# Decode attention: keys read in runs of 32, one exp a pair, and low parts made by an identity matmul

## The chip, the cores and the metric

The kernel runs on one core of a Trainium2 chip. The metric is the device time of one execution in microseconds, lower is better. Five executions of the kernel before gave 324.24 to 327.63 us, with a median of 326.44 us.

## The reference

Four tokens (B = 4, one query position each) of width 448 go through two identical layers. Each layer is attention over a cached window, then a SwiGLU FFN, both with a layer norm ahead and a residual behind. The caches and the weights are the same in both layers.

```python
B, Sq, D = 4, 1, 448
Hq, Hkv, Sk, Dh = 16, 8, 8192, 256
W = min(4096, max(256, Sk // 4))                       # 2048 keys
q = (x @ wq).reshape(B, Sq, Hq, Dh).transpose(0, 2, 1, 3)
k = jnp.repeat(k_cache[:, :, Sk - W:, :], rep, axis=1)  # rep = 2 query heads a key head
v = jnp.repeat(v_cache[:, :, Sk - W:, :], rep, axis=1)
scores = jnp.einsum("bhqd,bhkd->bhqk", q, k) * (Dh ** -0.5)
o = jnp.einsum("bhqk,bhkd->bhqd", _softmax(scores), v)
A = o.transpose(0, 2, 1, 3).reshape(B, Sq, Hq * Dh) @ wo
Bf = (_silu(x @ w_gate) * (x @ w_up)) @ w_down          # F = 1792

x = x + A(_layernorm(x)); x = x + Bf(_layernorm(x))     # twice
```

All inputs are bf16. For each token and key head the window holds 1 MB of keys and 1 MB of values, so one layer over four tokens reads 64 MB of cache.

## The kernel before

**Pairs and steps.** The unit of work is a pair: one token, one layer, one key head with its two query heads. There are 64 pairs. A window's keys come as two halves of 512 KB, and so do its values; each half is one tile of 128 partitions by 2048 bf16, out of a pool of 27 (`half`). Five of the eight key heads' K and V of a token's first layer stay in the pool until its second layer uses them, so 44 of the 64 pairs load their cache and 20 do not. `steps` joins a pair of one token's second layer with a pair of the next token's first layer for the same head, and the output projection is done once for both.

**A pair, in the order of its data** (function `pair`):

- SP issues the loads of K (L616) and V (L629).
- DVE transposes each K half in place, in 32 x 32 blocks of 32-bit words (L621), so a word holds two neighbouring elements of a key's head dimension.
- GpSimd spreads the query into four masked copies (L646, `qe`).
- TensorE makes the scores (L642, `scores`): 32 matmuls with a stationary operand of 128 x 8 and 128 moving columns, that is 32 keys of each of two by two places in a half. They go to four strips of 32 partitions of a PSUM bank `S` in turn, so a strip holds one quarter of the keys. There are two such banks (NS = 2).
- DVE takes the maximum (L653), TensorE passes it to all strips (L656), DVE reduces it and forms the bias of the exp (L660, L664).
- ScalarE makes the exp out of the bank `S` in two instructions, one for each half of the partitions (L668). They write to different columns of `praw`, and the columns in between stay zero.
- TensorE turns the probabilities so that keys are on partitions (L677, `turn`: 2 matmuls against `selt`), ScalarE copies them to SBUF (L684, `pT`), TensorE sums them (L687) and DVE reduces the sum (L692).
- TensorE multiplies by V (L700, `pv`: 32 matmuls of 256 columns in two halves) into a bank `Y`, columns 256 to 511. There are three such banks (NY = 3).
- Eviction: each result stands on several rows of `Y`, of which some are to carry the bf16 rounding of it and others the remainder. ScalarE copies the whole to bf16 (L712, `oh`). DVE multiplies `oh` by `lomask` and subtracts `Y` (L714), which leaves the negative of the value on some rows and of the remainder on the others.
- TensorE flips and adds the rows (L720, `flip`, against `osel`, which holds the minus sign), DVE multiplies by the inverse of the sum (L725, `oT`), and TensorE adds the projection into a bank `A` (L745, `out_proj`).

At the end of a token's layer come the residual (L563), the norm (L425 to L453), the FFN (gate and up L523, down L551) and, between the layers, the query projection (L482).

**Order.** Nothing is ordered by hand. Every operation is entered into a graph with an engine, a planned duration in us and a rank. `schedule` plays the graph once with these durations and so fixes the order of the instructions on every engine's queue, the order of the loads on SP's queue, and which tile of the pool a load gets. A tile is free again when the last reader is done: the scores for a K half (`o.rel = tuple(kc)`), the matmuls by V for a V half. On the chip each engine takes its queue strictly in this order and waits on semaphores. The planned durations of the operations that matter here:

```python
            o = g.op(PE, 32 * MM, pos - SLEAD, scores, r=tuple(kk) + (f"qe{q_}",), w=(f"s{s_}",), bank=(f"S{s_}",))
```

with MM = 0.034, 0.33 for an exp, 0.08 for the turn, 0.28 for L712 and 0.4 for L714.

Of the kernel before, what the change touches and what calls it, by code (L numbers as in the profile page):

```python
# [6 lines left out]
ALU = mybir.AluOpType  # L7
# [271 lines left out]
def build(nc, A_x, A_k_cache, A_v_cache, A_wq, A_wo, B_x, B_w_gate, B_w_up, B_w_down, out):  # L279
# [3 lines left out]
    with ExitStack() as es:  # L283
# [10 lines left out]
        onesb = sb("onesb", [128, 1], BF16)  # L294
# [3 lines left out]
        selt = sb("selt", [128, 2, 4, 2, 2], BF16)  # L298
# [8 lines left out]
        qmask = sb("qmask", [128, 4], BF16)  # L307
# [13 lines left out]
        pmax = [sb(f"pmax{s}", [128, 1], BF16) for s in range(NS)]  # L321
        praw = [sb(f"praw{s}", [128, 256], BF16) for s in range(NS)]
        pT = [sb(f"pT{s}", [128, 2, 2, 4, 2, 2], BF16) for s in range(NY)]
        oh = [sb(f"oh{s}", [128, DH], BF16) for s in range(NY)]
        osel = sb("osel", [128, 2], BF16)
# [41 lines left out]
        for y in range(2):  # L367
            for x in range(2):
                g.op(DVE, 0.1, R0, lambda e, y=y, x=x: e.tensor_reduce(
                    selt[:, x, :, y, :], ivt[:, :, x, 0:4, :].rearrange("p h a n -> p a n h"), AX.X, ALU.max),  # L370
                    r=("identb",), w=(f"selt{y}{x}",))
# [3 lines left out]
        for s_ in range(NS):  # L375
            g.op(DVE, 0.2, R0, lambda e, s_=s_: e.memset(Sb[s_][:, :], 0.0), w=(f"s{s_}",), bank=(f"S{s_}",))
            g.op(DVE, 0.2, R0, lambda e, s_=s_: e.memset(praw[s_][:, :], 0.0), w=(f"praw{s_}_0", f"praw{s_}_1"))
        for a in range(4):
# [4 lines left out]
            osel[:, :], iv[:, :, 0:2, :].rearrange("p j y n -> p n j y"), AX.XY, ALU.max, negate=True), r=("identb",),  # L383
            w=("osel",))
        g.op(DVE, 0.2, R0, lambda e: e.tensor_reduce(lomask[:, :], iv[:, :, 1, :], AX.XY, ALU.add), r=("identb",),
# [222 lines left out]
        def pair(pos, si, side, nside, t, layer, kvh):  # L608
# [26 lines left out]
            def scores(e):  # L635
                last = None
                for ce in range(8):
                    for hf in range(2):
                        kt = half[kc[hf][0]][:, :].rearrange("p (l g c r v) -> p c v g r l", l=2, g=4, c=4, v=2)
# [10 lines left out]
            o = g.op(PE, 32 * MM, pos - SLEAD, scores, r=tuple(kk) + (f"qe{q_}",), w=(f"s{s_}",), bank=(f"S{s_}",))  # L650
# [16 lines left out]
            for hf in range(2):  # L667
                g.op(SCA, 0.33, pos, lambda e, hf=hf: e.activation(  # L668
                    praw[s_][64 * hf:64 * hf + 40, :].rearrange("p (g r h l) -> p h g r l", g=2, h=2, l=2)[:, hf, :, :, :],
                    Sb[s_][64 * hf:64 * hf + 40, 0:128].rearrange("p (g r l) -> p g r l", g=2, l=2), ACT.Exp,  # L670
                    bias=nb[64 * hf:64 * hf + 40, 0:1]),
                    r=(f"s{s_}", f"nb{s_}"), w=(f"praw{s_}_{hf}",), bank=(f"S{s_}",))

            def turn(e):
                last = None
                for c in range(2):
                    last = e.matmul(Yb[p_][:, 64 + 32 * c:96 + 32 * c], lhsT=praw[s_][0:104, 128 * c:128 * c + 128],  # L677
                                    rhs=selt[0:104, :, :, :, :].rearrange("p x a y n -> p (x a y n)"), start=(c == 0),
                                    stop=False, skip_group_check=True)
                return last  # L680
            g.op(PE, 0.08, pos, turn,
                 r=(f"praw{s_}_0", f"praw{s_}_1") + tuple(f"selt{y}{x}" for y in range(2) for x in range(2)), w=(f"yp{p_}",),
                 bank=(f"Y{p_}",))
# [20 lines left out]
            for hv in range(2):  # L704
# [3 lines left out]
                if not keep_v:  # L708
# [3 lines left out]
            g.op(SCA, 0.28, pos, lambda e: e.activation(oh[p_][:, :], Yb[p_][:, 256:512], ACT.Copy), r=(f"y{p_}",),  # L712
                 w=(f"oh{p_}",), bank=(f"Y{p_}",))
            g.op(DVE, 0.4, pos, lambda e: e.scalar_tensor_tensor(  # L714
                out=oh[p_][:, :], in0=oh[p_][:, :], scalar=lomask[:, 0:1], in1=Yb[p_][:, 256:512], op0=ALU.mult,
# [128 lines left out]
```

## Time and profile before

| | us |
|---|---|
| median of five executions | 326.44 (324.24 to 327.63) |
| the profiled execution's own time | 326.44 |
| its span, first to last instruction | 324.6 |
| TensorE matmuls busy | 238.9 (74%), 5792 instructions |
| TensorE weight loads busy | 168.7 (52%) |
| VectorE (DVE) busy | 198.9 (61%) |
| ScalarE (ACT) busy | 91.1 (28%) |
| GpSimd (POOL) busy | 85.5 (26%) |
| loads' queue, share of the 16 DMA engines | 86.5%, 104.45 MB |
| mean granted TensorE clock | 0.763 |

How to read the lines of the profile: PE is TensorE's matmuls, PEld its weight loads, which overlap them. A matmul's busy time includes its way through the array, so matmuls that follow each other overlap, and a busy PE is not PE at its peak. In the slices the span is cut in 40 equal parts, and a digit is a share in tenths. In the chain, the work that ended last is followed back from the last instruction, at each step to what released it. In the groups, the columns are line, engine, operation, output and inputs, shapes and count, then busy time in us, the mean of one in ns, and the engine's idle time before them with what ended it. SPq is SP's queue, on which all loads are issued.

### The profile page before, as it was taken

Reading aid. Unit: us, or ns where it says so; the run is one execution under the profiler, and the core shown is the slowest. Engines: PE = TensorE matmul, PEld = TensorE weight load, DVE = VectorE, ACT = ScalarE, POOL = GpSimd, SP = SyncE. Lnnn points to the kernel's source line nnn. Section 1 sums busy time; section 2 is a strip of 40 time slices with the busy share of each in tenths; the row PEclk is TensorE's granted clock in tenths of the full one; section 3 lists DMA queues with packets and bytes.
Section 4 is the critical chain, followed back from the end, with each engine's and each line's share of the span. In section 5 each row is a group of like instructions: output and inputs, shape, how many; then the busy total and the mean of one; then the engine's idle time right before and its main releaser. Section 6 shows DMA issues by size and latency. Waiting matters only on the chain.

```text
span 324.6 us, 13161 instructions
## 1 busy us (share of the span) xinstructions
PE 238.9 (74%) x5792; PEld 168.7 (52%) x5792; DVE 198.9 (61%) x744; ACT 91.1 (28%) x289; POOL 85.5 (26%) x199
## 2 busy tenths in 40 slices
PE   2666565456587877688969976799878878689965
PEld 1543333234465545466735644566645547566644
DVE  6397556653145789675547997656567973944422
ACT  0313122111013344223243334222333433124510
POOL 2413211112020333223215232404142324134321
PEclk9998556777556999775597999655759978569965
DMA  7999999999988999998899999999599999736000
GB/s 274 404 404 392 395 396 394 392 397 397 392 319 291 389 372 374 363 365 293 298 367 397 399 380 298 390 389 391 179 397 359 331 388 392 274 103 231 2 2 2
DMA packets 42328, 105.28 MB, mean 324 GB/s; under 512 B 3096, under 2 KB 7200, under 8 KB 41888
## 3 DMA queue, kind: packets, MB, share of 16 engines
q1 hardware_dynamic: 42272, 104.45, 86.5%
q8 instruction: 45, 0.74, 0.9%
q14 instruction: 11, 0.09, 0.1%
HBM read 104.44 MB, written 0.00 MB: 322 GB/s over the span
## 4 chain that ended last, share of the span: by engine, by line
PE 39%; DMA 21%; DVE 16%; SPq 12%; issue 5%; ACT 5%
DMA half<-in_A_v_cache_dram 15%; PE S L642 15%; DVE half L621 8%; PE Y L700 8%; DMA half<-in_A_k_cache_dram 6%; SPq L616 6%; PE Z L482 4%; PE A L745 4%; SPq L629 3%; SPq L398 3%; ACT praw L668 3%; PE Z L523 2%; DVE oh L714 2%; ACT oh L712 1%; PE Y L720 1%
## 5 line engine op out<-in xcount | busy, mean ns | idle before, releaser
L621 DVE STREAM_TRANSPOSE half<-half 128x1024 uint32<-128x1024 uint32 x88 | 108.9, 1239 | 21.0 <-DMA half<-in_A_k_cache_dram 20.8
L642 PE MATMUL S<-half,qe 128*8 128x128 bf16 x2048 | 85.0, 306 | 9.2 <-ACT praw L668 5.0
L700 PE MATMUL Y<-half,pT 128*4 128x256 bf16 x1024 | 54.4, 330 | 20.6 <-DMA half<-in_A_v_cache_dram 12.2
L642 PEld LDWEIGHTS S<-half,qe 128*8 128x8 bf16 x2048 | 51.7, 90 | 28.3 <-ACT praw L668 8.4
L710 POOL TENSOR_TENSOR small<-small 128x2 f32<-128x2 f32 x64 | 44.4, 698 | 78.8 <-DVE small L692 71.5
L668 ACT ACTIVATE praw<-S,small 40x128 bf16<-40x128 f32 x128 | 46.4, 363 | 48.0 <-DVE small L664 46.4
L712 ACT ACTIVATE oh<-Y 128x256 bf16<-128x256 f32 x64 | 24.4, 381 | 86.4 <-PE Y L700 86.0
L646 POOL TENSOR_TENSOR qe<-qc,qmask 128x64 bf16<-128x64 bf16 x64 | 18.7, 294 | 101.0 <-PE S L642 85.1
L653 DVE TENSOR_REDUCE pmax<-S 104x1 bf16<-104x128 f32 x64 | 18.4, 288 | 38.0 <-PE S L642 37.7
L714 DVE SCALAR_TENSOR_TENSOR oh<-oh,small,Y 128x256 bf16<-128x256 bf16 x64 | 30.1, 472 | 17.1 <-ACT oh L712 16.9
L700 PEld LDWEIGHTS Y<-half,pT 128*4 128x4 bf16 x1024 | 21.5, 88 | 28.8 <-DMA half<-in_A_v_cache_dram 14.1
L745 PE MATMUL A<-oT,wo_sb 128*128 128x1 bf16 (+1 forms) x688 | 24.3, 165 | 6.8 <-DVE oT L725 5.1
L745 PEld LDWEIGHTS A<-oT,wo_sb 128*128 128x128 bf16 x688 | 20.9, 99 | 13.1 <-DVE oT L725 7.2
L684 ACT ACTIVATE pT<-Y 128x64 bf16<-128x64 f32 x64 | 13.9, 222 | 42.2 <-PE Y L677 30.1
L720 PE MATMUL Y<-osel,oh 128*128 128x2 bf16 x128 | 12.1, 170 | 13.0 <-DVE oh L714 13.0
L687 PE MATMUL Y<-pT,onesb 128*128 128x32 bf16 x64 | 12.0, 190 | 9.6 <-ACT pT L684 9.5
L720 PEld LDWEIGHTS Y<-osel,oh 128*128 128x128 bf16 x128 | 7.5, 102 | 21.4 <-DVE oh L714 17.1
L449 POOL TENSOR_SCALAR st<-st 128x1 f32<-128x1 f32 x16 | 4.3, 267 | 47.9 <-DVE st L437 36.7
L482 PE MATMUL Z<-xn,wq_sb 128*128 128x1 bf16 (+1 forms) x480 | 15.4, 166 | 1.0 <-DMA wq_sb<-in_A_wq_dram 0.7
L687 PEld LDWEIGHTS Y<-pT,onesb 128*128 128x128 bf16 x64 | 6.8, 107 | 16.0 <-ACT pT L684 12.5
L656 PE MATMUL S<-identb,pmax 104*104 104x32 bf16 x64 | 13.1, 223 | 2.5 <-DVE pmax L653 1.0
L482 PEld LDWEIGHTS Z<-xn,wq_sb 128*128 128x128 bf16 x480 | 14.2, 104 | 1.5 <-DMA wq_sb<-in_A_wq_dram 0.8
(81 smaller groups left out, 231.8 us busy)
## 6 DMA issues: line engine op xcount, KB each, us to landing
half<-in_A_k_cache_dram SPq DMA_DIRECT2D x88, 512.0 KB, 7.0
half<-in_A_v_cache_dram SPq DMA_DIRECT2D x88, 512.0 KB, 7.1
wo_sb<-in_A_wo_dram SPq DMA_DIRECT2D x8, 448.0 KB, 12.3
wq_sb<-in_A_wq_dram SPq DMA_DIRECT2D x3, 1024.0 KB, 6.9
wd_sb<-in_B_w_down_dram SPq DMA_DIRECT2D x1, 1568.0 KB, 16.3
wg_sb<-in_B_w_gate_dram SPq DMA_DIRECT2D x1, 1344.0 KB, 14.2
wu_sb<-in_B_w_up_dram SPq DMA_DIRECT2D x1, 1344.0 KB, 14.7
wq_sb<-in_A_wq_dram SPq DMA_DIRECT2D x1, 512.0 KB, 10.5
```

Of the source, the lines that this page charges most:

```text
L482: last = e.matmul(o, lhsT=lhsT, rhs=rhs, start=(cc == 0 and hh == 0 and ee == 0), stop=(cc == 3), skip_group_check=True)
L616: g.dma(pos - KLEAD, 1 << 19, lambda e, cell=cell, hf=hf: e.dma_start(half[cell[0]][:, :], ksrc[:, 2048 * hf:2048 * hf + 2048]), None, w=( ...
L621: return e.transpose(a, a)
L642: last = e.matmul(Sb[s_][qd:qd + 8, 0:128], lhsT=qe[q_][:, ce, :, :].rearrange("p a n -> p (a n)"), rhs=kt[:, ce // 2, ce % 2, 2 * x:2 * x ...
L668: g.op(SCA, 0.33, pos, lambda e, hf=hf: e.activation(praw[s_][64 * hf:64 * hf + 40, :].rearrange("p (g r h l) -> p h g r l", g=2, h=2, l=2 ...
L687: g.op(PE, 0.05, pos, lambda e: e.matmul(Yb[p_][:, 32:64].rearrange("p (k n) -> p k n", n=2), lhsT=onesb[:, 0:1].broadcast_to([128, 128]), ...
L700: last = e.matmul(Yb[p_][32 * gg:32 * gg + 4, 256:512], lhsT=pT[p_][:, gg % 2, gg // 2, 2 * hv + a, :, :].rearrange("p y n -> p (y n)"), r ...
L710: g.op(POOL, 0.25, pos, lambda e: e.tensor_tensor(ri[p_][:, :], rs[p_][:, :], expo[:, 1:3], op=ALU.pow), r=(f"rs{p_}", "expo"), w=(f"ri{p_ ...
L712: g.op(SCA, 0.28, pos, lambda e: e.activation(oh[p_][:, :], Yb[p_][:, 256:512], ACT.Copy), r=(f"y{p_}",), w=(f"oh{p_}",), bank=(f"Y{p_}",))
L714: g.op(DVE, 0.4, pos, lambda e: e.scalar_tensor_tensor(out=oh[p_][:, :], in0=oh[p_][:, :], scalar=lomask[:, 0:1], in1=Yb[p_][:, 256:512], ...
L720: last = e.matmul(Yb[p_][:, 2 * dh:2 * dh + 2], lhsT=oh[p_][:, :].rearrange("p (m e) -> p e m", e=2)[:, dh, :], rhs=osel[:, :], start=Fals ...
L745: last = e.matmul(Av[:, cc, sl], lhsT=wo_sb[:, 4 * kvh + k, c0:c0 + 128], rhs=oT[si % 2][:, k % 2, k // 2, 0:n], start=False, stop=False, ...
```

## The change

The transposed keys stay as they are; only the order in which the scores read them changes. Where the moving operand ran over group g, then row r, and innermost over two places l, it now runs over g, then l, and innermost over 32 rows r. So the columns of the bank `S` are in the order (g, l, r), and the exp reads them back in the order (g, r, l) that `praw` has.

The exp is one instruction for all 104 partitions instead of two for 40 each. It writes the same columns on all of them. The two halves are told apart by the turn: it has four matmuls instead of two, each with a `selt` of one half, and the window on `praw` is shifted by two columns for one of the halves (`praw` has two more columns for that).

The eviction does not use DVE. ScalarE copies `Y` times `lomask` (now negative) to `oh`, which is minus the rounded value on some rows and zero on the others. A matmul against the identity adds this to `Y` in PSUM, and ScalarE copies the outcome to `oh`. So `osel` has no minus sign any more.

Some small tiles are put together into one (`tiny`), `selt` becomes two tiles, and the planned durations follow: 0.8 for the scores, 0.38 for the exp, 0.12 for the turn, 0.38 and 0.22 and 0.38 for the eviction.

```diff
-        selt = sb("selt", [128, 2, 4, 2, 2], BF16)
+        selt = [sb(f"selt{h}", [128, 2, 4, 2, 2], BF16) for h in range(2)]
...
-        for y in range(2):
-            for x in range(2):
-                g.op(DVE, 0.1, R0, lambda e, y=y, x=x: e.tensor_reduce(
-                    selt[:, x, :, y, :], ivt[:, :, x, 0:4, :].rearrange("p h a n -> p a n h"), AX.X, ALU.max),
-                    r=("identb",), w=(f"selt{y}{x}",))
+        for h in range(2):
+            for y in range(2):
+                for x in range(2):
+                    g.op(DVE, 0.1, R0, lambda e, h=h, y=y, x=x: e.tensor_copy(selt[h][:, x, :, y, :], ivt[:, h, x, 0:4, :]),
+                         r=("identb",), w=(f"selt{h}{y}{x}",))
...
-            osel[:, :], iv[:, :, 0:2, :].rearrange("p j y n -> p n j y"), AX.XY, ALU.max, negate=True), r=("identb",),
+            osel[:, :], iv[:, :, 0:2, :].rearrange("p j y n -> p n j y"), AX.XY, ALU.max), r=("identb",),
...
-        g.op(DVE, 0.2, R0, lambda e: e.tensor_reduce(lomask[:, :], iv[:, :, 1, :], AX.XY, ALU.add), r=("identb",),
+        g.op(DVE, 0.2, R0, lambda e: e.tensor_reduce(lomask[:, :], iv[:, :, 1, :], AX.XY, ALU.add, negate=True), r=("identb",),
...
-                        kt = half[kc[hf][0]][:, :].rearrange("p (l g c r v) -> p c v g r l", l=2, g=4, c=4, v=2)
+                        kt = half[kc[hf][0]][:, :].rearrange("p (l g c r v) -> p c v g l r", l=2, g=4, c=4, v=2)
...
-            o = g.op(PE, 32 * MM, pos - SLEAD, scores, r=tuple(kk) + (f"qe{q_}",), w=(f"s{s_}",), bank=(f"S{s_}",))
+            o = g.op(PE, 0.8, pos - SLEAD, scores, r=tuple(kk) + (f"qe{q_}",), w=(f"s{s_}",), bank=(f"S{s_}",))
...
-            for hf in range(2):
-                g.op(SCA, 0.33, pos, lambda e, hf=hf: e.activation(
-                    praw[s_][64 * hf:64 * hf + 40, :].rearrange("p (g r h l) -> p h g r l", g=2, h=2, l=2)[:, hf, :, :, :],
-                    Sb[s_][64 * hf:64 * hf + 40, 0:128].rearrange("p (g r l) -> p g r l", g=2, l=2), ACT.Exp,
-                    bias=nb[64 * hf:64 * hf + 40, 0:1]),
-                    r=(f"s{s_}", f"nb{s_}"), w=(f"praw{s_}_{hf}",), bank=(f"S{s_}",))
+            g.op(SCA, 0.38, pos, lambda e: e.activation(
+                praw[s_][0:104, 2:258].rearrange("p (g r h l) -> p h g r l", g=2, h=2, l=2)[:, 0, :, :, :],
+                Sb[s_][0:104, 0:128].rearrange("p (g l r) -> p g r l", g=2, l=2), ACT.Exp, bias=nb[0:104, 0:1]),
+                r=(f"s{s_}", f"nb{s_}"), w=(f"praw{s_}",), bank=(f"S{s_}",))
...
                 for c in range(2):
-                    last = e.matmul(Yb[p_][:, 64 + 32 * c:96 + 32 * c], lhsT=praw[s_][0:104, 128 * c:128 * c + 128],
-                                    rhs=selt[0:104, :, :, :, :].rearrange("p x a y n -> p (x a y n)"), start=(c == 0),
-                                    stop=False, skip_group_check=True)
+                    for h in range(2):
+                        c0 = 128 * c + 2 - 2 * h
+                        last = e.matmul(Yb[p_][:, 64 + 32 * c:96 + 32 * c], lhsT=praw[s_][0:104, c0:c0 + 128],
+                                        rhs=selt[h][0:104, :, :, :, :].rearrange("p x a y n -> p (x a y n)"),
+                                        start=(c == 0 and h == 0), stop=False, skip_group_check=True)
...
-            g.op(SCA, 0.28, pos, lambda e: e.activation(oh[p_][:, :], Yb[p_][:, 256:512], ACT.Copy), r=(f"y{p_}",),
-                 w=(f"oh{p_}",), bank=(f"Y{p_}",))
-            g.op(DVE, 0.4, pos, lambda e: e.scalar_tensor_tensor(
-                out=oh[p_][:, :], in0=oh[p_][:, :], scalar=lomask[:, 0:1], in1=Yb[p_][:, 256:512], op0=ALU.mult,
-                op1=ALU.subtract), r=(f"y{p_}", f"oh{p_}", "lomask"), w=(f"oh{p_}",), bank=(f"Y{p_}",))
+            g.op(SCA, 0.38, pos, lambda e: e.activation(oh[p_][:, :], Yb[p_][:, 256:512], ACT.Copy, scale=lomask[:, 0:1]),
+                 r=(f"y{p_}", "lomask"), w=(f"oh{p_}",), bank=(f"Y{p_}",))
+            g.op(PE, 0.22, pos, lambda e: e.matmul(Yb[p_][:, 256:512], lhsT=identb[:, :], rhs=oh[p_][:, :], start=False,
+                                                   stop=False, skip_group_check=True),
+                 r=(f"oh{p_}", "identb"), acc=(f"y{p_}",), bank=(f"Y{p_}",))
+            g.op(SCA, 0.38, pos, lambda e: e.activation(oh[p_][:, :], Yb[p_][:, 256:512], ACT.Copy),
+                 r=(f"y{p_}",), w=(f"oh{p_}",), bank=(f"Y{p_}",))
```

## The prediction

> **What bounds the kernel now.** I read the page's slices first, then the table of stretches, the chain of waits, the groups by form, and last the timeline for single durations. Time is the profiled execution's: 326.4 us, of which the span is 324.6, and 1.8 lies around it; it is also the median of the runs shown (324.2 to 327.6).
>
> ```profile
> DMA  7999999999988999998899999999599999736000
> GB/s 274 404 404 392 395 396 394 392 397 397 392 319 291 389 372 374 363 365 293 298 367 397 399 380 298 390 389 391 179 397 359 331 388 392 274 103 231 2 2 2
> ```
>
> ```profile
> core 0: us, PE busy (x) PEld busy (x) DVE busy (x) ACT busy (x) POOL busy (x), PEclk, DMA share, GB/s
> 0.00:95.00 95.00, 53.08 (x1196) 38.50 (x1197) 51.52 (x188) 17.68 (x55) 19.74 (x52) 0.73 1.01 385
> 95.00:285.00 190.00, 154.45 (x3784) 107.19 (x3782) 133.40 (x477) 62.31 (x198) 54.86 (x122) 0.78 0.94 347
> 285.00:314.00 29.00, 25.27 (x648) 17.45 (x645) 11.46 (x66) 10.64 (x34) 9.25 (x20) 0.85 0.29 93
> 314.00:324.60 10.60, 6.13 (x176) 5.57 (x176) 2.48 (x16) 0.44 (x2) 1.66 (x5) 0.50 0.01 2
> ```
>
> Up to 95 us loads run at 385 GB/s and compute waits for them: a faster pair is worth nothing there. From 95 to 285 us loads fall to 347 GB/s, with holes in the slices: buffers come free too late, so compute sets part of the pace. Up to 314 us the last eight pairs are compute alone; the rest is the final FFN, untouched. The change can act on 95 to 314 us, 219 us with 53 pairs, whose chain is:
>
> ```profile
> by line: PE S L642 20.7%; DVE half L621 11.6%; PE Y L700 10.5%; DMA half<-in_A_k_cache_dram 8.9%; DMA half<-in_A_v_cache_dram 7.5%; issue 6.4%; PE A L745 5.1%; PE Z L482 4.8%; ACT praw L668 4.5%; DVE oh L714 2.8%; DVE pmax L653 1.7%; ACT oh
> ```
>
> PE holds some 45% of it (41% in the four lines named), DVE 18%, DMA 16%. The scores (L642) are the largest piece: 45.3 us.
>
> **Scores: the new order of the moving operand.** Two stretches of the table, for L642 and then L700 alone: the sums of four at the full clock and of four at half.
>
> ```profile
> sum 102.40, PE 40.65 PEld 23.86; mean PE 10.16 PEld 5.97
> sum 92.10, PE 18.32 PEld 11.60; mean PE 4.58 PEld 2.90
> ...
> sum 102.40, PE 19.69 PEld 9.98; mean PE 4.92 PEld 2.50
> sum 92.10, PE 19.02 PEld 6.31; mean PE 4.75 PEld 1.58
> ```
>
> L642 ran 996 matmuls in the first and 436 in the second: 40.8 and 42.0 ns each. L700 (526 and 272) took 37.4 and 69.9 ns. So PV follows the granted clock and the scores do not: something other than the array paces them. L642 reads keys as l, the innermost index, alternating between two places 2 KB apart; L700 reads 256 neighbours.
>
> The Trainium skill ("Advanced Engine Details and Errata", SBUF Cachelines) says SBUF is read in 16-byte lines and that a new line on every access costs. Here that fits the missing dependence on the clock, and four keys of the new run share a line; by the rule the scores would fall to the array's pace.
>
> How far they fall I take from the timeline:
>
> ```profile
> 208.59 1.28 PE L523 MATMUL Z<-xn,wg_sb 128*128 128x2 bf16 x42 [0.53 <-DVE st L437]
> 210.39 1.31 PE L642 MATMUL S<-half,qe 128*8 128x128 bf16 x32
> ```
>
> Matmuls with almost no columns, each with a weight load, go every (1.28 − 0.165) / 41 = 27 ns; the scores every (1.31 − 0.306) / 31 = 32 ns. I take 27. The last matmul's own time lies between 165 ns (2 columns) and 330 (256, L700): 248 for 128, against 306. A block then takes 31 × 0.027 + 0.248 = 1.085 us, 0.225 less. The chain holds 45.3 / 1.31 = 34.6 blocks: **−7.8 us**. Bounds: 0, if the order does not matter; or, if four strips go together as in PV at the full clock, half of its 4 × 37.4 ns a group, 8 × 0.075 + 0.248 = 0.85 us a block: −16. A 4-byte step, which stays, shows no cost in weight loads (L482 104 ns with it, L551 104 without).
>
> **One exp instead of two.** The rows for this and the eviction:
>
> ```profile
> L668 ACT ACTIVATE praw<-S,small 40x128 bf16<-40x128 f32 x128 | 46.4, 363 | 48.0 <-DVE small L664 46.4
> L714 DVE SCALAR_TENSOR_TENSOR oh<-oh,small,Y 128x256 bf16<-128x256 bf16 x64 | 30.1, 472 | 17.1 <-ACT oh L712 16.9
> L712 ACT ACTIVATE oh<-Y 128x256 bf16<-128x256 f32 x64 | 24.4, 381 | 86.4 <-PE Y L700 86.0
> L684 ACT ACTIVATE pT<-Y 128x64 bf16<-128x64 f32 x64 | 13.9, 222 | 42.2 <-PE Y L677 30.1
> L490 ACT ACTIVATE qS<-Z,st 128x4 bf16<-128x4 f32 x8 | 2.1, 264 | 9.2 <-PE Z L482 7.6 <-POOL st L453 1.3
> L490 ACT ACTIVATE qS<-Z,st 128x16 bf16<-128x16 f32 x8 | 1.5, 275 | 5.5 <-PE Z L482 5.5
> ```
>
> ACT's time goes with elements a partition, (381 − 222) / 192 = 0.83 ns, so one exp over 104 partitions costs 0.363 and one of two falls away. The chain holds 4.5% × 219 = 9.9 us of them: **−4.9 us**. New is a stepped read of PSUM. L490's sixteen elements, four floats apart, cost 11 ns more than four: 0.9 ns each, no penalty. Bounds: −4.9, and −3.5 if it read at half pace (13.6 × 0.106 us back).
>
> The same page (PSUM Cachelines) speaks against this: PSUM's lines are 8 bytes, and patterns that are not contiguous slow matmuls strongly. By it taken over to ScalarE this term would be the −3.5; L490's row goes against that.
>
> **The eviction.** Out goes L714, 0.472 us on DVE. In come a scale by pointer on the first copy (264 against 222 − 60 × 0.83 = 172 ns: +0.09), a 256-column matmul (0.33, by L700's mean) and a second copy (0.381), with one more handover (0.05 between L700's end and L712). Where this is on the chain, 6.1 / 0.472 = 13 times, it adds 0.85 and removes 0.472: **+5.0 us**. For the 40 other pairs the matmul fills PE's queue for 4 × 54.4 / 1024 = 0.21 us, of which PE's 45% counts: **+3.8**; its bounds are 0 (in an idle gap) and 8.4. The turn's two extra matmuls, 53 × 0.054 × 0.45: **+1.3**. DVE gets back, from 95 us on, 25.8 us of L714 and 15.5 us in which it stood still for L712, less the 6.1 counted; 18% of 35: **−6.3**, bounds 0 and −15. ACT's net +0.11 a pair lies in its idle time (62 of 190 us busy); without that cover it is 6 us. Behind the new matmul's wait on PE stand the scores of later pairs, PV and the projection, and behind these the release of K and V buffers and so SP's loads: that is the danger.
>
> At the start, eight small copies for selt replace four reductions, some 0.7 us more on DVE. They lie in the load-bound first stretch, where every pair waits for its loads; uncovered they cost 0.7. The planner gets new durations and may reorder all queues, SP's too. No row prices that; the hole of 4.8 us at 284.7 us, when no load runs, may close or open as wide: ±4.8, taken as 0.
>
> **Sum.** −7.8 − 4.9 + 5.0 + 3.8 + 1.3 − 6.3 = −8.9 us. A shorter chain soon meets the loads, which already hold 16% of it and can give back at most (1 − 347/385) × 190 = 19 us. I count two thirds, a choice: −5.9, or **320.5 us**. All of it gives 317.5, one third 323.5.
>
> **Rivals.** *The order of reading is not the limit*, and the change's main part does nothing: the sum is −1.1, the time 325.7. For it: no row shows a moving operand in the new order. Against: the 40.8 and 42.0 ns at clocks two to one apart.
> *PE waits twice.* PE takes its queue in order and now stops for ScalarE before the identity matmul and again before the flip (L720). Today it stood idle 13.0 us before the flip, 24 times: 0.54 us each. One such wait more in the 40 pairs off the chain, at PE's 45%, is +9.7: 330.2 us, slower. For it: legs of half a microsecond are shorter than a score block that could fill them. Against: ScalarE idles two thirds of the time and answers at once, where DVE had 1.24 us transposes ahead of the subtraction. It decides from 13 us of extra idle time on PE (5.9 / 0.45), so when PE is idle more than 26 us before the two.
> *Loads catch up*: the scores go at PV's pace, DVE's relief frees K earlier, loads keep 385 GB/s: −19, 307.6 us. For it: the holes all lie where PE and DVE are dense. Against: seven buffers are left when five K and five V pairs are held.
>
> **How the numbers follow.** Forecast (314 to 323) 0.47; catching up (305 to 314) 0.15; no effect 0.15; PE waits 0.23. One per cent, about what a measurement here tells from no change, is 3.3 us: faster 0.62, same 0.15, slower 0.23. The forecast's own range is 314 to 323; with the unknown bounds, 310 to 331.
>
> **What would show it.** Right: L642 near 34 ns a matmul (block 1.1 us); L668 64 times at 0.36 us; DVE below 172 us busy; the slices between 95 and 285 us above 355 GB/s. Wrong: a score block still at 1.3 us; an exp of 0.45 us; over 26 us of PE idle before the identity matmul and the flip; holes in the loads as wide as now although blocks are shorter.

## The result and the profile after

The change makes no difference that can be measured. Over many executions of both kernels the time after is 1.0012 times the time before, with a 95% interval of 0.9994 to 1.003: at 327.6 us before that is 0.4 us more. The forecast was 5.9 us less. The profiled execution of after took 331.98 us, above its median of 328.35; such executions are left out of the ratio, and so this profile is read for durations, counts and the clock, not for its span.

The groups of the kernel after that answer to those shown of before (line numbers have moved by up to two; the second copy and the identity matmul are new):

```profile
L641 PE MATMUL S<-half,qe 128*8 128x128 bf16 x2048 | 64.7, 293 | 17.7 <-DVE half L620 9.3 <-issue 5.4 <-ACT praw L666 2.0
L699 PE MATMUL Y<-half,pT 128*4 128x256 bf16 x1024 | 65.2, 380 | 8.3 <-DMA half<-in_A_v_cache_dram 5.0 <-DVE small L691 1.9 <-DVE st L427 1.0
L711 ACT ACTIVATE oh<-Y,small 128x256 bf16<-128x256 f32 x64 | 30.3, 474 | 96.3 <-PE Y L699 96.3
L716 ACT ACTIVATE oh<-Y 128x256 bf16<-128x256 f32 x64 | 24.3, 383 | 37.5 <-PE Y L713 32.9 <-PE Y L686 3.3 <-PE S L655 1.0
L713 PE MATMUL Y<-oh,identb 128*128 128x256 bf16 x64 | 23.2, 368 | 8.5 <-ACT oh L711 8.4
L666 ACT ACTIVATE praw<-S,small 104x128 bf16<-104x128 f32 x64 | 22.3, 365 | 23.6 <-DVE small L663 23.0
```

The rows of the kernel before for the scores and for PV:

```profile
L642 PE MATMUL S<-half,qe 128*8 128x128 bf16 x2048 | 85.0, 306 | 9.2 <-ACT praw L668 5.0
L700 PE MATMUL Y<-half,pT 128*4 128x256 bf16 x1024 | 54.4, 330 | 20.6 <-DMA half<-in_A_v_cache_dram 12.2
```

Most single prices are as forecast. The scores are 20 us less busy (85.0 before), the one exp takes 365 ns, the scaled copy 474 and the plain one 383, and VectorE is 174 us busy instead of 199. What was not forecast is the second row of after: PV, which the change does not touch, went from 54.4 to 65.2 us busy.

The slices of after, and its table for the stretch that compute sets, show why:

```profile
PEclk9999999999999555555558555555555576557955
GB/s 279 394 406 392 394 396 393 393 398 390 395 253 304 400 399 366 337 355 250 343 286 357 402 365 348 382 378 370 258 395 350 322 337 401 240 61 263 5 0 4
...
core 0: us, PE busy (x) PEld busy (x) DVE busy (x) ACT busy (x) POOL busy (x), PEclk, DMA share, GB/s
95.00:285.00 190.00, 161.26 (x3825) 111.58 (x3817) 113.21 (x415) 63.77 (x198) 53.31 (x118) 0.57 0.94 344
```

Between 95 and 285 us the granted clock is 0.57; it was 0.78. (The record of the clock begins 100 us into the span here, and the page counts the time before it as full. PV's matmuls in the first 95 us take 404 ns on average, against 272 in before's stretch at full clock from 102 to 133 us, so by their length the clock was half. With the 5.6 us from 95 us on counted as half, the 0.57 is 0.55.) The loads run at 344 GB/s, where they ran at 347: nothing of the relief reached them.

The scores and PV of after by clock, first at full clock (four stretches, 256 and 204 matmuls), then at half (two, 1216 and 592):

```profile
sum 30.60, PE 5.29 PEld 3.69; mean PE 1.32 PEld 0.92
sum 153.60, PE 40.72 PEld 29.56; mean PE 20.36 PEld 14.78
...
sum 30.60, PE 8.18 PEld 3.03; mean PE 2.04 PEld 0.76
sum 153.60, PE 39.30 PEld 12.81; mean PE 19.65 PEld 6.41
```

The scores now follow the clock as PV does: 20.7 ns each at full clock and 33.5 at half, against 41 and 42 before. PV takes 40.1 and 66.4 ns. Half clock makes a matmul of the scores 1.6 times as long and one of PV 1.7 times. So the old order of reading was the limit, and with the new one the array's clock sets the pace; but that clock is mostly half.

The chain of after for its own compute stretch (95 to 319 us; PE's lines are L641, L699, L713, the loads are the DMA entries):

```profile
by line: PE S L641 18.0%; DMA half<-in_A_k_cache_dram 17.9%; PE Y L699 16.2%; DMA half<-in_A_v_cache_dram 6.7%; issue 6.1%; PE Z L481 4.7%; PE Y L713 4.4%; DVE half L620 4.0%; PE A L746 3.8%; PE Z L522 3.8%; PE Y L721 1.8%; ACT oh L711 1.5%
```

Before, DVE's transposes and subtraction held 14.4% of this and the loads 16.4%. Now DVE's transposes hold 4.0%, and PV (10.5% before) with the identity matmul holds 20.6%, the loads 24.6%. These are shares of one execution: with the same queues, the run below with a narrow identity matmul shows 8.9% for the transposes (95 to 314 us), and the run with the old order of the scores 11.8% for the loads.

### The profile page after: what moved, and what is told of

It is laid out like the page before. It is cut to its first block, busy times and chain, and to the rows that moved or that the text cites. A ratio compares the mean times of both kernels' runs of the same rounds, so it can differ in the third digit from the quotient of the medians.

```text
span 330.0 us, 13492 instructions
## 1 busy us (share of the span) xinstructions
PE 252.2 (76%) x5984; PEld 177.4 (54%) x5984; DVE 174.4 (53%) x684; ACT 93.1 (28%) x289; POOL 85.4 (26%) x199
## 4 chain that ended last, share of the span: by engine, by line
PE 51%; DMA 23%; DVE 11%; issue 5%; SPq 5%; ACT 4%
DMA half<-in_A_k_cache_dram 16%; PE S L641 14%; PE Y L699 13%; DVE half L620 8%; DMA half<-in_A_v_cache_dram 7%; PE Z L481 4%; PE Z L522 4%; PE Y L713 4%; PE A L746 3%; SPq L615 2%; ACT oh L711 2%; ACT oh L716 2%; PE Y L721 2%; SPq L397 2%; SPq L628 1%
## 5 line engine op out<-in xcount | busy, mean ns | idle before, releaser
L620 DVE STREAM_TRANSPOSE half<-half 128x1024 uint32<-128x1024 uint32 x88 | 108.3, 1237 | 15.9 <-DMA half<-in_A_k_cache_dram 15.6
L641 PE MATMUL S<-half,qe 128*8 128x128 bf16 x2048 | 64.7, 293 | 17.7 <-DVE half L620 9.3
L699 PE MATMUL Y<-half,pT 128*4 128x256 bf16 x1024 | 65.2, 380 | 8.3 <-DMA half<-in_A_v_cache_dram 5.0
L641 PEld LDWEIGHTS S<-half,qe 128*8 128x8 bf16 x2048 | 46.8, 112 | 25.0 <-DVE half L620 10.6
L711 ACT ACTIVATE oh<-Y,small 128x256 bf16<-128x256 f32 x64 | 30.3, 474 | 96.3 <-PE Y L699 96.3
L652 DVE TENSOR_REDUCE tiny<-S 104x1 bf16<-104x128 f32 x64 | 18.4, 288 | 45.6 <-PE S L641 45.3
L645 POOL TENSOR_TENSOR qe<-qc,tiny 128x64 bf16<-128x64 bf16 x64 | 18.7, 294 | 85.6 <-PE S L641 71.5
L699 PEld LDWEIGHTS Y<-half,pT 128*4 128x4 bf16 x1024 | 20.7, 95 | 20.1 <-DMA half<-in_A_v_cache_dram 7.5
L713 PE MATMUL Y<-oh,identb 128*128 128x256 bf16 x64 | 23.2, 368 | 8.5 <-ACT oh L711 8.4
L666 ACT ACTIVATE praw<-S,small 104x128 bf16<-104x128 f32 x64 | 22.3, 365 | 23.6 <-DVE small L663 23.0
L721 PE MATMUL Y<-tiny,oh 128*128 128x2 bf16 x128 | 13.3, 173 | 7.9 <-ACT oh L716 7.5
L691 DVE TENSOR_REDUCE small<-Y 128x2 f32<-128x32 f32 x64 | 10.8, 177 | 12.5 <-PE Y L686 12.1
L676 PE MATMUL Y<-selt,praw 104*128 104x32 bf16 x256 | 17.1, 189 | 0.0
## 6 DMA issues: line engine op xcount, KB each, us to landing
wq_sb<-in_A_wq_dram SPq DMA_DIRECT2D x1, 512.0 KB, 10.5
```

The source lines that it names most:

```text
L620: return e.transpose(a, a)
L641: last = e.matmul(Sb[s_][qd:qd + 8, 0:128], lhsT=qe[q_][:, ce, :, :].rearrange("p a n -> p (a n)"), rhs=kt[:, ce // 2, ce % 2, 2 * x:2 * x ...
L645: g.op(POOL, 0.25, pos - SLEAD - 1, lambda e: e.tensor_tensor(qe[q_][:, :, :, :], qc[t][:, kvh, :, :].unsqueeze(2).broadcast_to([128, 8, 4 ...
L666: g.op(SCA, 0.38, pos, lambda e: e.activation(praw[s_][0:104, 2:258].rearrange("p (g r h l) -> p h g r l", g=2, h=2, l=2)[:, 0, :, :, :], ...
L699: last = e.matmul(Yb[p_][32 * gg:32 * gg + 4, 256:512], lhsT=pT[p_][:, gg % 2, gg // 2, 2 * hv + a, :, :].rearrange("p y n -> p (y n)"), r ...
L711: g.op(SCA, 0.38, pos, lambda e: e.activation(oh[p_][:, :], Yb[p_][:, 256:512], ACT.Copy, scale=lomask[:, 0:1]), r=(f"y{p_}", "lomask"), w ...
```

## The experiments

All ratios are to the kernel before, measured beside each kernel; intervals are 95%, and the uncertainty given with a difference is the half width of its interval. One per cent is 3.3 us. Kernels with the same operations and planned durations have the same order on every queue; these pairs are the clean comparisons. In all kernels the order of the loads on SP is the same, but the tiles are not: `schedule`, played with the durations of before and of after, gives 66 of the 176 loads of halves another tile and lets 30 of them wait for another reader.

In the kernels with the new order of the scores, the record of the clock begins 100 to 131 us into the span, and the tables count the time before it as full. PV's matmuls there are as long as at half clock (between 95 us and the first record 408 ns on average in the scores alone, with PV whole). A clock in brackets counts that time as half; it is an estimate from these lengths.

**The scores alone, in before's queues.**

```diff
-  kt = half[...].rearrange("p (l g c r v) -> p c v g r l", ...)
+  kt = half[...].rearrange("p (l g c r v) -> p c v g l r", ...)
-  Sb[s_][64 * hf:64 * hf + 40, 0:128].rearrange("p (g r l) -> p g r l", ...)
+  Sb[s_][64 * hf:64 * hf + 40, 0:128].rearrange("p (g l r) -> p g r l", ...)
```

> The kernel before with only the order changed in which the scores read the keys, and the two exps reading S in that order; planned durations and so all queues are as before. Theory A (clock): a block of scores falls from 1.31 us to about 1.03 at half clock and 0.63 at full clock, TensorE is less active, its granted clock between 95 and 285 us falls from 0.78 to 0.65 or less, PV rises from 54 us busy to 60 or more, and the time is 322 to 327 us. Theory B (eviction: the loss of the whole change is in the identity matmul and TensorE's waits for ScalarE): the clock stays above 0.73, PV at 54 us, and the time falls by the 6 to 8 us that the scores were priced at, 319 to 321 us. Theory C (the loads hide everything): time within 1 us of before, clock unchanged.

Measured: 0.9943 (0.9914 to 0.9972), 1.9 us less. Its table for the stretch and its two groups:

```profile
95.00:285.00 190.00, 150.86 (x3815) 108.83 (x3813) 133.97 (x480) 62.81 (x199) 54.87 (x123) 0.63 0.94 347
...
L700 PE MATMUL Y<-half,pT 128*4 128x256 bf16 x1024 | 64.5, 381 | 24.4 <-DMA half<-in_A_v_cache_dram 11.7 <-DVE small L692 7.6 <-issue 4.9
L642 PE MATMUL S<-half,qe 128*8 128x128 bf16 x2048 | 63.7, 292 | 8.7 <-DVE half L621 5.0 <-ACT praw L668 2.2 <-issue 0.7
```

Every instruction stands where it stood; the scores read the keys, and the exps the bank `S`, in another order. The scores give up 21 us, PV takes on 10, and the clock goes from 0.78 to 0.63 (0.57). This is what theory A expected. TensorE as a whole is only 6 us less busy (232.8 for 238.9).

**After with the scores in the old order**, first with their old planned duration too, then with after's, so in after's queues.

The last two lines of the diff are in the first of the two alone.

```diff
-  kt = half[...].rearrange("p (l g c r v) -> p c v g l r", ...)
+  kt = half[...].rearrange("p (l g c r v) -> p c v g r l", ...)
-  Sb[s_][0:104, 0:128].rearrange("p (g l r) -> p g r l", ...)
+  Sb[s_][0:104, 0:128].rearrange("p (g r l) -> p g r l", ...)
...
-  o = g.op(PE, 0.8, pos - SLEAD, scores, ...)
+  o = g.op(PE, 32 * MM, pos - SLEAD, scores, ...)
```

> The kernel after with the scores in the old order of reading (and their old planned duration); one exp, four turn matmuls and the eviction through TensorE stay. Theory A: the granted clock between 95 and 285 us comes back to 0.73 or more, PV falls from 65 to about 55 us, and the time is within 1% of after (326 to 330 us), since what the slower scores cost comes back in all other matmuls. Theory B: the time rises by the price of the scores, to 333 us or more. Theory C: no change from after.

> The kernel after with the scores read in the old order, but with the planned duration of after, so that every queue is after's: the pure effect of the reading order in after's queues. Theory A (the faster scores lower the clock, and most of their gain is paid back): clock between 95 and 285 us 0.75 or more, PV 51 to 56 us, scores 85 us busy, time 328 to 331 us, 1 to 2 us above after, as in before's queues, where the new order gave 1.9 us. If the 4.6 us of the earlier run with old scores came from its own queue order (theory D), this run is clearly below it, at 1.001 to 1.008 of before. If the order is worth its full price: 1.014 or more.

Measured: 1.0139 (1.0093 to 1.0185) and 1.0079 (1.0045 to 1.0112). The clock is back at 0.83 and 0.79, PV at 50.7 and 53.1 us. Of the second run:

```profile
95.00:285.00 190.00, 161.16 (x3870) 110.72 (x3863) 116.25 (x430) 63.15 (x198) 53.88 (x121) 0.79 0.95 347
...
L699 PE MATMUL Y<-half,pT 128*4 128x256 bf16 x1024 | 53.1, 321 | 5.6 <-DMA half<-in_A_v_cache_dram 2.4 <-DVE small L691 1.9 <-DVE st L427 0.7
```

The second run against after (1.0012) is the order of reading alone in after's queues: 0.67%, 2.2 us, the same as in before's. The first run comes near theory B's number, but 2 us of it are its own queue order, since the two kernels have the same instructions. The first run shares its queues with a kernel further below, after with before's planned duration for the scores (1.0054). Against that one the order of reading is worth 0.85%, 2.8 us. So three sets of queues give 1.9, 2.2 and 2.8 us, with uncertainties of 1.0, 1.2 and 2.0.

**The eviction alone, and taken out of after.** The first is before with this diff (and the signs of `lomask` and `osel` that go with it), the second is after with the same diff the other way round.

```diff
-  g.op(SCA, 0.28, pos, lambda e: e.activation(oh[p_][:, :], Yb[p_][:, 256:512], ACT.Copy), ...)
-  g.op(DVE, 0.4, pos, lambda e: e.scalar_tensor_tensor(out=oh[p_][:, :], in0=oh[p_][:, :], scalar=lomask[:, 0:1], ...), ...)
+  g.op(SCA, 0.38, pos, lambda e: e.activation(oh[p_][:, :], Yb[p_][:, 256:512], ACT.Copy, scale=lomask[:, 0:1]), ...)
+  g.op(PE, 0.22, pos, lambda e: e.matmul(Yb[p_][:, 256:512], lhsT=identb[:, :], rhs=oh[p_][:, :], start=False, ...), ...)
+  g.op(SCA, 0.38, pos, lambda e: e.activation(oh[p_][:, :], Yb[p_][:, 256:512], ACT.Copy), ...)
```

> The kernel before with only the eviction of after (scaled copy, identity matmul, second copy). Theory A: the clock between 95 and 285 us stays at 0.75 or more, VectorE is 24 us less busy, and the time is within 1% of before (324 to 330 us). Theory B: TensorE idles over 26 us ahead of the identity matmul and the flip, and the time is 332 us or more. Theory C: within 1 us of before.

> The kernel after with the old eviction (one copy on ScalarE, the subtraction on VectorE, no identity matmul); new order of the scores, one exp and four turn matmuls stay. Theory A: the granted clock between 95 and 285 us stays at 0.55 to 0.65, or is lower still as TensorE has less to do, and the time is 322 to 328 us. Theory B: 316 to 321 us. Theory C: as after.

Measured: alone 0.992 (0.9888 to 0.9952), 2.6 us less, with the clock at 0.79 and VectorE 24 us less busy; TensorE stood idle 13.5 us before the identity matmul and the flip together. After without it: 0.9906 (0.9872 to 0.994), 3.1 us less, with the clock at 0.58 (0.56). So the eviction gains by itself, and costs 3.5 us beside the other two parts. Each of these kernels has queues of its own; what that does to such a comparison is told below.

**One matmul more, to hold the clock up**, on after and on the scores alone.

```diff
   def scores(e):
       last = None
+      e.matmul(Sb[s_][:, 160:512], lhsT=identb[:, :], rhs=esel[...][:, 0:352], start=False, stop=False, ...)
```

> The kernel after with one more matmul ahead of each block of scores, in the same operation, so that every queue keeps its order: 128x128 against 352 constant columns, into columns of the bank S that nobody reads. It is pure extra work for TensorE: 0.15 us at full clock and 0.29 us at half, 9 to 19 us in all. Theory A (the granted clock fell because the scores got short): the clock between 95 and 285 us rises from 0.57 to 0.75 or more, PV falls from 65 to 56 us or less, and the time does not rise; it falls to 320 to 326 us. If the clock is only a by-product and not a cause: the clock may rise, but the time is 331 us or more.

> The kernel before with the new order of the scores alone, queues as before, plus the same extra matmul of 352 columns ahead of each block of scores. Theory A: the clock between 95 and 285 us rises from 0.63 to 0.75 or more, PV falls from 64 to 56 us or less, a block of scores takes 0.63 us in most cases, and the time falls from 325 to 319 to 323 us. If the clock is no cause: 327 us or more.

Measured: 1.0232 (1.0169 to 1.0295) and 1.0055 (1.0017 to 1.0093). The clock came to 0.68 (0.63) and 0.61 (0.57) only, from 0.57 (0.55) and 0.63 (0.57). Both expectations of theory A failed, and the times are those of the other case. But one such matmul a pair doesn't bring the clock back, so these two runs don't say what a higher clock would be worth; the extra matmul's own time is paid.

**Three such matmuls on the scores alone.**

> The kernel before with the new order of the scores, queues as before, and three extra matmuls of 352 columns ahead of each block of scores instead of one: 0.44 us at full clock, 0.88 at half. If the clock follows the time in which columns stream through TensorE: the clock between 95 and 285 us comes to 0.75 or more, PV below 56 us, and the time stays within 1% of the run with one extra matmul (1.0055). If the extra matmuls do nothing to the clock: below 0.68, PV above 60 us, and 1.02 or more of before.

Measured: 1.0221 (1.0167 to 1.0275). Table and groups of this kernel (L638 is the extra matmul):

```profile
95.00:285.00 190.00, 160.25 (x3788) 102.68 (x3786) 129.29 (x456) 62.08 (x196) 53.21 (x118) 0.73 0.93 338
...
L703 PE MATMUL Y<-half,pT 128*4 128x256 bf16 x1024 | 55.4, 339 | 6.0 <-DVE small L695 3.9 <-issue 1.2 <-DMA half<-in_A_v_cache_dram 0.5
L638 PE MATMUL S<-esel,identb 128*128 128x352 bf16 x192 | 54.7, 410 | 14.7 <-DVE half L621 9.5 <-ACT praw L671 4.7 <-DVE xs L563 0.2
L645 PE MATMUL S<-half,qe 128*8 128x128 bf16 x2048 | 54.5, 263 | 1.6 <-issue 1.6
```

Now the clock is 0.73 (0.72), PV is back at 55 us and the scores are at 54.5. So it is TensorE's own activity that moves the clock. But 55 us of extra work bring back 9 us of PV and 9 of scores, and the time is 2.8% above the scores alone. Of the expectation, PV came as it said and the clock nearly; the time did not, and lies where the other case put it. The clock can be bought here, at a loss.

**PV cut to its former busy time.**

```diff
-  last = e.matmul(Yb[p_][32 * gg:32 * gg + 4, 256:512], ..., rhs=half[...][:, 1024 * a + 256 * gg:1024 * a + 256 * gg + 256], ...)
+  last = e.matmul(Yb[p_][32 * gg:32 * gg + 4, 256:448], ..., rhs=half[...][:, 1024 * a + 256 * gg:1024 * a + 256 * gg + 192], ...)
```

> The kernel before with the new order of the scores, queues as before, and PV on 192 of its 256 columns (a quarter of the head's outputs is left out). At half clock this brings PV back from 64 us busy to about 52, near its 54 in the kernel before. If the time that PV lost to the low clock is what took the scores' gain (theory A): 0.984 to 0.989 of before, 2 to 3 us below the run with whole PV. If TensorE's time there lies beside other work: 0.991 to 0.997, no change.

Measured: 0.9886 (0.9839 to 0.9933), 1.9 us below the whole PV (0.9943), with PV at 54.9 us and the clock at 0.59 (0.51):

```profile
95.00:285.00 190.00, 148.65 (x3831) 112.50 (x3824) 134.09 (x479) 62.96 (x199) 55.06 (x123) 0.59 0.94 347
...
L700 PE MATMUL Y<-half,pT 128*4 128x192 bf16 x1024 | 54.9, 348 | 25.3 <-DMA half<-in_A_v_cache_dram 12.8 <-issue 6.7 <-DVE small L692 5.3
```

By theory A's numbers this lies in its range (0.984 to 0.989), at the edge of it, and the interval reaches into the other. The 1.9 us carry an uncertainty of 1.8. Taken at their value, PV at its old busy time would have made the scores' gain 3.7 us instead of 1.9; that is an estimate, since this PV is narrower and not faster.

**The exp and the turn alone; then after with two exps and two turns, in after's queues.**

The first is before with the exp (one, 104 partitions) and the turn (four matmuls) of after. The second is after with this diff.

```diff
-  g.op(SCA, 0.38, pos, lambda e: e.activation(praw[s_][0:104, 2:258]..., Sb[s_][0:104, 0:128]..., ACT.Exp, ...), ...)
+  def exps(e):
+      for hf in range(2):
+          last = e.activation(praw[s_][64 * hf:64 * hf + 40, 0:256]..., Sb[s_][64 * hf:64 * hf + 40, 0:128]..., ACT.Exp, ...)
+      return last
+  g.op(SCA, 0.38, pos, exps, ...)
...
-      for h in range(2):
-          last = e.matmul(..., lhsT=praw[s_][0:104, c0:c0 + 128], rhs=selt[h][...], ...)
+      last = e.matmul(..., lhsT=praw[s_][0:104, 128 * c:128 * c + 128], rhs=selt[0][...], ...)
```

> The kernel before with the one exp and the four turn matmuls alone; old order of the scores, old eviction. By the prediction's terms (minus 4.9 for the exp, plus 1.3 for the turn, two thirds of it) 324 us, with the clock as before (0.75 or more). If the exp and the turn are what costs the whole change its gain, since the eviction without them was 2.6 us faster and with them 4.6 us slower than before: 331 us or more, with TensorE idle longer ahead of the turn. If that was only the order of the queues that the planner made: within 2 us of before.

> The kernel after with two exps of 40 partitions and two turn matmuls as in before, each pair of them in one operation with the planned duration of after, so that every queue is after's. It differs from after in ScalarE's second exp (0.36 us a pair more) and in two turn matmuls a pair less. By the prediction's terms after's single exp is worth 4.9 less 1.3 us, two thirds of it: 330 to 332 us. If one exp with four turn matmuls gains nothing, as the run with these alone (0.998) says: within 1.5 us of after.

Measured: 0.9984 (0.9937 to 1.0031) and 0.995 (0.9911 to 0.9989). The second is 0.62% below after: in after's queues the single exp with its four turn matmuls costs 2.0 us, with an uncertainty of 1.4. Neither case of its expectation had that sign. The first came out as its third case, within 2 us of before.

**The turn by itself**: after, and then the kernel with the exp and the turn alone, each with two of the four turn matmuls.

```diff
-  for h in range(2):
+  for h in range(1):
       c0 = 128 * c + 2 - 2 * h
```

> The kernel after with two of the four turn matmuls (half of the keys' weights is left out, so the probabilities and sums are not the reference's); one exp, all queues as after. If the two added turn matmuls are the 2 us that the single exp cost: 0.993 to 0.997 of before, as with two exps and two turns. If the single exp itself or its place is the cost: 1.000 to 1.004, as after.

> The kernel before with one exp and with two of the four turn matmuls that it needs (half of the keys' weights is left out, so the probabilities and sums are not the reference's); old order of the scores, old eviction; queues as in the run with the exp and all four turn matmuls, which was 0.998 of before. If the turn's two added matmuls cost 3 to 5 us wherever they stand: 0.983 to 0.990. If their price in after came from the low clock or from the identity matmul beside them: 0.994 to 1.000.

Measured: 0.985 (0.9808 to 0.9893) and 0.9993 (0.9956 to 1.0031). In after's queues the two added matmuls cost 1.6%, 5.3 us, with an uncertainty of 1.5; that is more than either case of the expectation. The group of the turn shows little of it, after first and then with two matmuls a pair:

```profile
L676 PE MATMUL Y<-selt,praw 104*128 104x32 bf16 x256 | 17.1, 189 | 0.0
...
L676 PE MATMUL Y<-selt,praw 104*128 104x32 bf16 x128 | 13.9, 192 | 0.6 <-DVE oT L726 0.3 <-ACT pT L683 0.3
```

That is 3.2 us of TensorE's time in all. In the other kernel, with old scores and old eviction, the same cut gives nothing. So the price is not the turn's as such, but that of 50 ns a pair in this kernel. The expectation put such an outcome down to the low clock or to the identity matmul beside the turn. The two kernels also differ in their queues, and no run separates the three. With two turns, one exp against two is 0.985 against 0.995, a gain of 3.3 us, with an uncertainty of 1.9.

**The identity matmul on 16 of its 256 columns.**

> The kernel after with the identity matmul on 16 of its 256 columns (the low parts of the others are left out); both copies, all waits and all queues as after. It takes some 0.2 us of 0.37 off each identity matmul, at the low clock 13 us in all on TensorE. If TensorE's time is what the eviction costs beside the scores: 0.990 to 0.996 of before, 2 to 3.5 us below after. If it is the chain of two copies and TensorE's waits: 0.998 to 1.003.

Measured: 0.9991 (0.9955 to 1.0026), 0.7 us below after, with an uncertainty of 1.3. The matmul went from 23.2 to 11.7 us busy (368 to 188 ns), so its time on TensorE is worth little here. That the chain of copies and waits is what remains of the eviction follows by exclusion; no run shows it.

**The order of the queues.** The scores and the eviction together, with the planned durations of these parts; after with measured durations planned (scores 1.0, scaled copy 0.48, identity matmul 0.37); after with before's duration for the scores (32 * MM); and before with after's, which is this diff:

```diff
-  o = g.op(PE, 32 * MM, pos - SLEAD, scores, ...)
+  o = g.op(PE, 0.8, pos - SLEAD, scores, ...)
```

> The kernel before with the new order of the scores and the new eviction; two exps and two turn matmuls stay as they were. If the parts add up (scores 1.9 us, eviction 2.6 us): 0.986 of before, 322 to 324 us. Theory A with theory B: at the low clock TensorE's added work in the eviction costs what the scores gain, 0.995 to 1.005. The clock between 95 and 285 us is 0.55 to 0.68 in both cases.

> The kernel after with nothing but the planned durations changed to measured ones (scores 1.0, scaled copy 0.48, identity matmul 0.37), so the same instructions in other queue orders; the order of the loads stays. Theory D (the order that the planner made with too short durations costs several us): 322 to 326 us. Theory A: the clock stays below 0.65 and the time is within 1% of after, 326 to 331 us.

> The instructions of after; only the planned duration of the scores is before's (1.088 in place of 0.8), which gives other queue orders; the order of the loads stays. Theory D (the order of the queues alone moves the time by several us): 2 us or more off after, to either side. If order does not matter: 326.5 to 329.5 us.

> The instructions of before; only the planned duration of the scores is after's (0.8 in place of 1.088), which gives other queue orders; the order of the loads stays. If the order of the queues moves the time by itself (0.4% to 0.6% between the runs of one program in two or three orders so far): 0.994 to 1.006 of before, and differences below some 2 us between kernels with queues of their own say nothing on the instructions. If the planner's order is worth more: outside that.

Measured: 0.995 (0.9915 to 0.9985); 1.0058 (1.0015 to 1.0101); 1.0054 (1.0014 to 1.0094); 1.0118 (1.0085 to 1.015). The first has the instructions of the kernel with two exps and two turns in after's queues, and the same time, in another order; its clock is 0.65 (0.57). The gains of scores and eviction, 1.9 and 2.6 us, do not add up in it: together they give 1.6. Planning with better durations did not make after faster: it is 1.5 us slower, with an uncertainty as large. Theory D's gain did not come. And before's own instructions lose 3.9 us when one planned duration is changed, which is outside the 0.994 to 1.006 expected. So two kernels with different queues can differ by 1.2% for the order alone, and the eviction's 2.6 us of gain alone and 3.5 of loss beside the rest are within that. Differences inside one set of queues are free of it.

## Why the prediction was wrong, point by point

The forecast was 5.9 us less and the result 0.4 more, a miss of 6.3 us. In after's queues the change can be taken apart. Two exps and two turns in after's queues hold the scores, the eviction and the order: −1.6 us. The scores are −2.2 of that, which leaves +0.6 for the eviction and the order together. The single exp is −3.3, the turn +5.3. The sum is the measured +0.4 by construction, since each step starts where the last one ends; each carries an uncertainty of 1.2 to 1.9 us. The prediction's terms, after its two thirds, were −5.2 for the scores, +1.7 for the eviction, −3.3 for the exp and +0.9 for the turn. So 4.4 us of the miss are the turn's and 3.0 the scores', and the eviction and the order take 1.1 off.

- **What bounds the kernel**: right. Loads set the first 95 us in both kernels at 385 GB/s.
- **Scores, the mechanism**: right. They did not follow the clock, and in the new order they do. A block was forecast at 1.085 us and is 1.03 at half clock and 0.63 at full, where the bound of four strips together (0.85) was passed too.
- **Scores, what it is worth**: this step failed. The sum held the clock fixed, and so put at nothing what the shorter block does to the other matmuls. With the shorter block TensorE is granted half clock in most of the compute stretch, and PV gives back 10 of the 21 us. The price was −5.2 and the runs show −1.9, −2.2 and −2.8. That the busy time comes back is shown; what it costs rests on one run: PV cut back returns 1.9 us, some 60% of the 3.3 missing there, and its uncertainty is nearly as large. Where the rest went is open. The loads' share of the chain grew from 16 to 25%, but it is 11.8% in after's queues with the old scores, so that they took it is not shown.
- **One exp**: −3.3 us forecast, −3.3 measured in after's queues with two turns; with an uncertainty of 1.9, so close a match is luck. The stepped read of PSUM costs nothing: 365 ns against 363.
- **Turn**: this step failed, and it is the larger part of the miss. It was priced by its 54 ns and by TensorE's share of the chain, +0.9 us after the two thirds. The length was right (3.2 us busy more for 64 pairs), and the runs show +5.3 in after's queues and nothing beside the old scores and the old eviction. A share of the chain is an average over a kernel; here it was the wrong measure in both directions. Why 50 ns a pair cost more than their own length in after is open.
- **Eviction and DVE's relief**: the durations were right (0.09 us for the scale; 368 ns for the identity matmul where 330 were forecast, and 324 in the run with the old scores, whose clock is 0.79). VectorE's busy time fell by 24.5 us, to 174.4, which is not below the 172 named as a sign. Net +1.7 was forecast; +0.6 is what is left over for it, with the order in it. In the chains shown, DVE's transposes fell from 11.6 to 4.0%, and PV and the loads took that place; the run with the narrow identity matmul, in the same queues, has 8.9%.
- **Planner**: set at 0 with ±4.8 us. That bound was fair: one duration in the plan moved before by 3.9 us. Taking 0 was a choice without a row behind it.
- **Rivals**: "the order of reading is not the limit" is refuted, though the time that it stood for, no change, came true: the scores did get shorter, and the rest of the change took that back. "PE waits twice" is refuted too: TensorE was idle 8.4 us before the identity matmul and 7.5 before the flip, 15.9 in all, where it was 13.0 before, against the 26 from which it would decide. "Loads catch up" did not happen: 344 GB/s.
- By the rule of the Trainium skill on SBUF's lines ("Advanced Engine Details and Errata", SBUF Cachelines) the scores fall to the array's pace. The 20.7 and 33.5 ns at the two clocks agree with it. No run tells a new line on every access from another cost of taking two places 2 KB apart in turn. The page's rule on PSUM's lines (PSUM Cachelines) speaks of matmuls, and by the 365 ns of the exp it did not carry over to ScalarE.

That no gain is left is then two things: a main part worth 2 us instead of 5, and an exp whose 3.3 us are more than spent by the turn that it needs here. The kernel after with the old eviction is ahead of both, 0.9906, though by no more than the order of queues can make; the scores' order alone, in before's queues, is ahead by 0.57% without that doubt.

## What to carry to other kernels

When a matmul is made shorter, look at what the granted clock will do, and price the other matmuls at half clock as well. The two rows of a group at the two clocks give that price before anything is built. Where a planner or a scheduler sets the order, change the instruction with the queues held first; a comparison across orders here carried up to 1.2% of its own. And an edit that needs a helper instruction on the path from one wait to the next has to be priced with that helper there, not by an average share.

## What the runs showed of the hardware

TensorE's clock is not granted for being busy by the profile's rows. After at half clock for 153.6 us, and before at full clock for 81.9 us:

```profile
sum 153.60, PE 133.22 PEld 91.84 DVE 93.67 ACT 51.10 POOL 44.22; mean PE 66.61 PEld 45.92 DVE 46.83 ACT 25.55 POOL 22.11
...
sum 81.90, PE 64.41 PEld 42.11 DVE 70.70 ACT 32.25 POOL 27.12; mean PE 21.47 PEld 14.04 DVE 23.57 ACT 10.75 POOL 9.04
```

PE is 87% busy in the first and 79% in the second. Part of the 87% is the half clock itself, at which a matmul of PV is busy for 66.4 ns instead of 40.1. The Trainium skill ("TensorE: Matmul & The Clock Gate", Part 1) says that a window of some 3.4 us of sustained activity releases the throttle. In these rows a busier TensorE is the one held at half clock. What would fit is the time in which columns stream: slow reading kept columns moving for 1.3 us a block and fast reading does not, three more matmuls of 352 columns a pair brought the clock from 0.63 (0.57) to 0.73 (0.72), and PV with a quarter of its columns left out took it to 0.59 (0.51). One more matmul in before's queues left it where it was (0.57). What decides the grant was not measured, so this stays a reading.

The moving operand's order can cost a factor of two at full clock: 41 ns a matmul with two places 2 KB apart taken in turn, 20.7 ns with runs of 32 at a step of 4 bytes.
